# A linear-attention and mish feed-forward kernel: both feed-forward products by seven block products for eight, in two parts

## The chip, the cores and the metric

The kernel runs on one core of one Trainium2 chip. The time is the device time of one execution in microseconds (us); each kernel is run several times and the median stands. A profile of one execution goes with it. The engines are TensorE (PE, with its weight loads as PEld), VectorE (DVE), ScalarE (ACT), GpSimd (POOL) and SyncE (SP, which here issues all DMAs).

## What is computed

```python
kv = np.einsum('bhsd,bhse->bhde', k, v)                   # 8 batches, 8 heads, 576 rows, 64 wide
o = np.einsum('bhsd,bhde->bhse', q, kv)
o = o / np.sqrt(np.mean(o * o, axis=-1, keepdims=True) + 1e-06) * g_norm
x = o.transpose(0, 2, 1, 3).reshape(4608, 512)
h = x @ w_in                                              # 512 x 2048
sp = np.where(h > 20.0, h, np.log1p(np.exp(np.minimum(h, 20.0))))
out = (h * np.tanh(sp)) @ w_out                           # 2048 x 512
```

q, k, v and g_norm come as float32, w_in and w_out as float64. The output is float32.

## The kernel before

**Precision.** A float32 product runs as three float32r passes. Each operand is split into a high part (a rounded copy, made by ACT) and a low part (the rest, a subtraction on DVE); `split` at L84 does both. The passes are low by high, high by low and high by high, so every block of a product is three matmuls. The weights arrive as pairs of 32-bit words of a float64; `weight` (L92) makes a float32 of them with one ACT scaling and three DVE bit operations, and splits it. All of w_in and w_out, high and low, stays in SBUF.

**Tiles.** The 4608 tokens are 9 tiles of 512. For each tile and each of four head pairs, `unit_steps` (L191) loads q in strips of 32 by 32 (eight or sixteen DMAs for one or two batches in the tile), transposes it on DVE, multiplies it with the block-diagonal k^T v of the pair (L215 for the first two tiles, L218 to L220 with split operands for the rest), squares, sums over the head by a matmul with ones (L234, L236, L237), takes Ln and Exp for the inverse root (L242, L243) and scales (L246). k^T v of a batch is `kv_product` (L149), from two halves of four heads that `kv_load` (L122) brings.

**Feed-forward.** `hidden` (L255) makes one of 16 chunks of 128 hidden features for the 512 tokens: 12 matmuls, each with 128 x 128 weights standing and 512 tokens moving (L259 to L261). Mish has no instruction of its own here: `mish_a` and `mish_b` (L266 to L282) build it from Exp, a bounded minimum, Square, Ln, Exp and two multiplications, and split the outcome. `project_out` (L284) multiplies each chunk of 128 hidden features with w_out into four PSUM banks of 128 tokens by 512: 12 matmuls per chunk (L288 to L290), with the mish outputs standing and w_out moving. A tile is thus 384 matmuls of 512 columns, and the kernel 3456. After the 16th chunk the four banks are copied (L293) and stored (L294).

**Order.** The string `START` (L18) orders the first tile's x and the first weights. The main loop (L369) goes through 9 x 16 chunks; the second product runs two chunks behind the first. `attention_slots` (L337) puts the steps to the next tile's x between the chunks. In the first tile each chunk also loads and converts one piece of w_in, as far as any is left, and one of w_out (L376 to L380). Tile, the framework, takes this program with its dependencies and orders each engine's instructions by a simulated schedule, so an engine's queue may run ahead of the program's order. Buffers in SBUF and PSUM are rings of a given depth (`bufs`); an instruction that takes a buffer waits for the last reader of what was in it.

Of the kernel before, what the change touches and what calls it, by code (L numbers as in the profile page):

```python
# [12 lines left out]
LB = -18 * 0.6931471805599453     # log(4 2^-20)  # L13
# [4 lines left out]
START = (  # L18
    "w0 k0 q0 q1 m0 t1 w1 t0 q2 s1 s0 c0 c1 w2 k1 m1 "
    "n1 t2 w3 n0 c2 w4 q3 s2 n2 c3 t3 s3 c4 w5 c5 n3"  # L20
)
# [3 lines left out]
def linear_attention_rms_mish_ffn(  # L25
# [20 lines left out]
    w_in, w_out = w_in.bitcast(U32), w_out.bitcast(U32)   # words of float64, low first  # L46
    P = 128
    T = 512                      # tokens of one tile of the feed-forward part
    NT = NTOK // T
    NKC = DM // P                # contraction chunks of x w_in, = head pairs  # L50
    NFC = DF // P                # chunks of the hidden dimension
    NSUB = T // P
# [7 lines left out]
    stage = ctx.enter_context(tc.tile_pool(name="stage", bufs=2))  # L60
    wraw = ctx.enter_context(tc.tile_pool(name="wraw", bufs=3))
    wstage = ctx.enter_context(tc.tile_pool(name="wstage", bufs=2))
    kvp = ctx.enter_context(tc.tile_pool(name="kvp", bufs=1))
    att = ctx.enter_context(tc.tile_pool(name="att", bufs=1))
# [27 lines left out]
    def weight(src, hi, lo):  # L92
        w = wraw.tile([P, T, 2], U32, name="w64")
        nc.sync.dma_start(w.rearrange("p n t -> p (n t)"), src)

        low, high = w[:, :, 0], w[:, :, 1]
        x = wstage.tile([P, T], F32, name="w32")

        def scale():
# [336 lines left out]
```

## Time and profile before

| what | value |
|---|---|
| median of three runs | 923.93 us (923.43 to 924.76) |
| profiled execution's own time | 924.76 us |
| its span | 924.8 us |
| DMA | 55.31 MB, mean 60 GB/s |
| mean granted TensorE clock | 0.986 |

How to read it: busy times are those of one profiled execution. Matmuls are pipelined and their durations overlap, so the pace is the distance from one start to the next in the timeline. PEld is the loading of the standing operand and lies beside PE. Where a group's row ends in "idle before, releaser", the number is the time that the engine sat idle just ahead of such instructions and what ended it. The chain of waits follows the last instruction back to what released each step.

### The profile page before, as it was taken

The numbers are of one execution on the slowest core, as the hardware profiler recorded it, in microseconds if no ns is written. First come the engines' busy times: TensorE is split into PE (matmuls) and PEld (weight loads), VectorE is DVE, ScalarE is ACT, GpSimd is POOL, SyncE is SP. The second block draws the span as 40 slices with busy tenths as digits, with TensorE's granted clock in tenths as the row PEclk, the third lists the DMA queues.
The fourth block names the chain that finished last, engine by engine and source line by source line (L and its number), as shares of the span: only waits on it lengthen the run. The fifth ranks groups of instructions, "written<-read, shape, count | busy, mean of one in ns | idle before, by whom it ended". The sixth has DMA issues, their size and how long they took to land.

```text
span 924.8 us, 11829 instructions
## 1 busy us (share of the span) xinstructions
PE 896.3 (97%) x4348; PEld 717.2 (78%) x4348; DVE 539.0 (58%) x908; ACT 635.4 (69%) x1057; POOL 0.2 (0%) x4
## 2 busy tenths in 40 slices
PE   3789999999999999999999999999999999999997
PEld 1467778888888888888788878888888888888886
DVE  5889986565456544655466545554565456544443
ACT  3688877677667766776577666776676677766554
POOL 0000000000000000000000000000000000000000
PEclk9779999999999999999999999999999999999999
DMA  8964361200250005200430034002300030001001
GB/s 217 276 210 138 107 232 45 47 1 1 70 122 4 1 3 129 63 0 1 117 78 1 1 103 91 1 1 74 69 1 1 1 88 5 0 1 46 1 1 45
DMA packets 113434, 55.31 MB, mean 60 GB/s; under 512 B 88288, under 2 KB 104672, under 8 KB 113376
## 3 DMA queue, kind: packets, MB, share of 16 engines
q1 hardware_dynamic: 113376, 54.55, 21.4%
q8 instruction: 34, 0.56, 0.2%
q14 instruction: 24, 0.20, 0.1%
HBM read 45.09 MB, written 9.44 MB: 59 GB/s over the span
## 4 chain that ended last, share of the span: by engine, by line
PE 94%; DMA 3%; SPq 1%; DVE 1%; ACT 1%; issue 0%; ACTq 0%
PE psh L259 15%; PE acc L290 15%; PE acc L288 14%; PE acc L289 14%; PE psh L261 14%; PE psh L260 14%; PE psa L157 3%; DMA w<-in_moe_w_in_dram 2%; PE psa L220 1%; PE psa L219 1%; DMA vm<-in_v_dram 1%; PE psa L218 1%; SPq L185 1%; PE psa L237 1%; PE psa L236 1%; PE psa L215 1%
## 5 line engine op out<-in xcount | busy, mean ns | idle before, releaser
L259 PE MATMUL psh<-xh,wil 128*128 128x512 f32 x576 | 231.2, 402 | 2.2 <-ACT xh L85 2.2
L260 PE MATMUL psh<-xl,wih 128*128 128x512 f32 x576 | 228.2, 396 | 0.0
L261 PE MATMUL psh<-xh,wih 128*128 128x512 f32 x576 | 227.9, 396 | 0.0
L290 PE MATMUL acc<-woh,gh 128*128 128x512 f32 x576 | 227.6, 395 | 0.0
L289 PE MATMUL acc<-wol,gh 128*128 128x512 f32 x576 | 227.2, 394 | 0.0
L288 PE MATMUL acc<-woh,gl 128*128 128x512 f32 x576 | 223.4, 397 | 0.0
L86 DVE TENSOR_TENSOR gl<-n,gh 128x512 fp32r<-128x512 f32 x144 | 99.5, 691 | 84.7 <-ACT gh L85 81.5
L278 DVE TENSOR_TENSOR n<-u,n 128x512 f32<-128x512 f32 x144 | 99.3, 690 | 82.5 <-ACT n L274 82.3
L85 ACT CAST gh<-n 128x512 fp32r<-128x512 f32 x144 | 89.1, 618 | 82.2 <-DVE n L278 67.2
L272 DVE SCALAR_TENSOR_TENSOR u<-u,psh 128x512 f32<-128x512 f32 x144 | 98.8, 686 | 76.9 <-ACT n L271 76.8
L269 ACT ACTIVATE u<-psh 128x512 f32<-128x512 f32 x144 | 86.2, 598 | 78.6 <-PE psh L261 77.6
L259 PEld LDWEIGHTS psh<-xh,wil 128*128 128x128 f32 x576 | 108.9, 189 | 29.6 <-ACT xh L85 2.6
L260 PEld LDWEIGHTS psh<-xl,wih 128*128 128x128 f32 x576 | 109.1, 189 | 26.3 <-issue 0.9
L261 PEld LDWEIGHTS psh<-xh,wih 128*128 128x128 f32 x576 | 108.7, 189 | 25.8 <-issue 0.2
L289 PEld LDWEIGHTS acc<-wol,gh 128*128 128x128 f32 x576 | 108.5, 188 | 25.2 <-ACT u L269 0.4
L290 PEld LDWEIGHTS acc<-woh,gh 128*128 128x128 f32 x576 | 108.2, 188 | 25.4 <-issue 0.2
L288 PEld LDWEIGHTS acc<-woh,gl 128*128 128x128 f32 x576 | 108.2, 188 | 25.4 <-issue 0.4
L271 ACT ACTIVATE n<-u 128x512 f32<-128x512 f32 x144 | 90.8, 631 | 44.0 <-DVE u L270 42.9
L274 ACT ACTIVATE n<-n,lb 128x512 f32<-128x512 f32 x144 | 104.1, 723 | 3.6
L273 ACT ACTIVATE n<-n,tiny 128x512 f32<-128x512 f32 x144 | 104.1, 723 | 3.2
L270 DVE TENSOR_SCALAR u<-u 128x512 f32<-128x512 f32 x144 | 61.2, 425 | 68.9 <-ACT u L269 68.2
L86 DVE TENSOR_TENSOR fl<-fa,fh 128x512 fp32r<-128x512 f32 x56 | 38.6, 689 | 19.3 <-ACT fh L85 18.7
(61 smaller groups left out, 569.1 us busy)
## 6 DMA issues: line engine op xcount, KB each, us to landing
out_dram<-stg SPq DMA_DIRECT2D x36, 256.0 KB, 2.0
w<-in_moe_w_in_dram SPq DMA_DIRECT2D x16, 512.0 KB, 4.9
km<-in_k_dram SPq DMA_DIRECT2D x16, 512.0 KB, 4.0
vm<-in_v_dram SPq DMA_DIRECT2D x16, 512.0 KB, 5.4
w<-in_moe_w_out_dram SPq DMA_DIRECT2D x16, 512.0 KB, 3.9
stg<-in_q_dram SPq DMA_DIRECT2D x32, 64.0 KB, 2.4
stg<-in_q_dram SPq DMA_DIRECT2D x32, 56.0 KB, 2.0
stg<-in_q_dram SPq DMA_DIRECT2D x32, 48.0 KB, 1.9
```

The lines of the kernel that those rows point to most:

```text
L86: nc.vector.tensor_sub(lo, src, hi.bitcast(F32))
L259: nc.tensor.matmul(ps, wil[:, kc, f], xh[:, kc, :], start=(kc == 0), stop=False)
L260: nc.tensor.matmul(ps, wih[:, kc, f], xl[:, kc, :], start=False, stop=False)
L261: nc.tensor.matmul(ps, wih[:, kc, f], xh[:, kc, :], start=False, stop=(kc == NKC - 1))
L271: nc.scalar.activation(r, v, AF.Square, bias=1.0, scale=2.0)
L272: nc.vector.scalar_tensor_tensor(v, v, 0.5, ps, ALU.add, ALU.mult)
L273: nc.scalar.activation(r, r, AF.Ln, bias=tiny, scale=2.0 ** -20)
L274: nc.scalar.activation(r, r, AF.Exp, bias=lb, scale=-1.0)
L278: nc.vector.tensor_mul(r, v, r)
L288: nc.tensor.matmul(acc[t], gl[:, c], woh[:, fc, :], start=first, stop=False)
L289: nc.tensor.matmul(acc[t], gh[:, c], wol[:, fc, :], start=False, stop=False)
L290: nc.tensor.matmul(acc[t], gh[:, c], woh[:, fc, :], start=False, stop=last)
```

## The change

**The algorithm.** Both feed-forward products go by Strassen's way in Winograd's form. The two operands are cut in two by two blocks; four sums of blocks on each side give seven forms a side, and seven block products stand for eight. `PROD` names them: left form, right form, PSUM bank. The blocks accumulate partly in PSUM: a bank is copied aside by ACT while it holds one product (c1, c5, c2), the next product accumulates onto it, and DVE adds a copy to the finished bank.

**Part 1** runs over 9 tiles of 512 tokens, 4 groups a tile. A left form is 256 features by 256 tokens of x; a right form 256 features by 256 hidden ones of w_in. A block product is 12 matmuls of 256 columns, and 7 products make a group. x itself is now kept in float32, its sums are formed on DVE, and each form is split. The attention steps go by two head pairs at once (1024 elements an instruction) and k and v by two heads a load. Mish is one ACT instruction, `AF.Mish`; `in_turn` chains the Mish, Ln and Exp instructions in program order, with a table load ahead of each Ln. The mish outputs go to HBM (`gd`, 4608 x 2048 float32), two stores a group.

**The weights.** `weight_forms` makes seven split forms of a chunk. w_in is 8 chunks of 1024 elements a partition, kept in the eight buffers `wfp` of 14 KB a partition. w_out is 16 half chunks of 512, of which tiles 1 to 8 make two each; their forms are stored to HBM (`wod`, 14.7 MB).

**Part 2** begins when part 1's pools are closed. The eight buffers of w_in take w_out's forms. 18 groups of 256 tokens follow: one load of mish outputs (2.1 MB), four sums, seven forms, seven products of 24 matmuls of 256 columns each, and one store of 256 x 512 outputs. The forms are made three products ahead.

The core of the diff:

```diff
-    "w0 k0 q0 q1 m0 t1 w1 t0 q2 s1 s0 c0 c1 w2 k1 m1 "
-    "n1 t2 w3 n0 c2 w4 q3 s2 n2 c3 t3 s3 c4 w5 c5 n3"
+START = "k0 q0 k1 w0 m0 t0 q1 w1 s0 m1 t1 r0 s1 c0 r1 w2 a0 f0 f1 a1 f2 f3 f4 f5 c1 c2 w3"
+A11, S1, S2, S4, A12, S3, A22 = range(7)
+T1, T3, T2, T4, B11, B22, B21 = range(7)
+PROD = ((A11, B11, "a"), (S1, T1, "c"), (A22, T4, "p"), (S2, T2, "a"), (S4, B22, "c"), (A12, B21, "b"), (S3, T3, "a"))
...
+    wfp = ctx.enter_context(tc.tile_pool(name="wfp", bufs=NF2))
+    ps_m = ctx.enter_context(tc.tile_pool(name="ps_m", bufs=2, space=PSUM))
+    cp = ctx.enter_context(tc.tile_pool(name="cp", bufs=1))
+    ps_t = part1.enter_context(tc.tile_pool(name="ps_t", bufs=1, space=PSUM))
+    big = part1.enter_context(tc.tile_pool(name="big", bufs=3))
...
+    def mish(o, i):
+        in_turn(nc.scalar.activation(o, i, AF.Mish))
...
+        def join():
...
+            nc.vector.tensor_single_scalar(t, t, 3, ALU.logical_shift_left)
+            nc.vector.scalar_tensor_tensor(t, high, 0x80000000, t, ALU.bitwise_and, ALU.bitwise_or)
+            nc.vector.scalar_tensor_tensor(t, low, 29, t, ALU.logical_shift_right, ALU.bitwise_or)
+        def differences():
...
+            nc.vector.tensor_sub(d[:, 0:2], x[:, 1:3], x[:, 0:2])
+            nc.vector.tensor_sub(d[:, 2], x[:, 2], d[:, 0])
+            nc.vector.tensor_sub(d[:, 3], x[:, 3], d[:, 2])
...
+        def first():
+            parts(T1, T4 + 1, st["d"])
+        def rest():
+            parts(B11, B11 + 1, st["x"][:, 0:1])
+            parts(B22, B21 + 1, st["x"][:, 2:4])
...
+        def rstd():
+            r = st["r"] = att.tile([P, 2, T], F32, name="fa")
+            in_turn(nc.scalar.preload_act_table_set("natural_log_exp_and_others"))
+            in_turn(nc.scalar.activation(r, st["ss"], AF.Ln, bias=eps, scale=1.0 / D))
+            in_turn(nc.scalar.activation(r, r, AF.Exp, scale=-0.5))
...
+    def group(st, mm, copy_shape, put, prev):
...
+        def p0():
+            st["a"] = st["bank"]("a")
+            mm(st, st["a"], A11, B11, True)
+            st["c1"] = c_tile("c1")
+            nc.scalar.copy(st["c1"], st["a"])
+        def p1():
+            st["c"] = st["bank"]("bc")
+            mm(st, st["c"], S1, T1, True)
+            st["c5"] = c_tile("c5")
+            nc.scalar.copy(st["c5"], st["c"])
+        def p2():
+            if prev is not None:
+                mm(prev, prev["a"], A22, T4, False)
+                put(prev, "21", prev["a"])
+        def p3():
+            mm(st, st["a"], S2, T2, False)
+            st["c2"] = c_tile("c2")
+            nc.scalar.copy(st["c2"], st["a"])
+        def p4():
+            mm(st, st["c"], S4, B22, False)
+            put(st, "12", st["c"], st["c2"])
+        def p5():
+            st["b"] = st["bank"]("bc")
+            mm(st, st["b"], A12, B21, True)
+            put(st, "11", st["b"], st["c1"])
+        def p6():
+            mm(st, st["a"], S3, T3, False)
+            put(st, "22", st["a"], st["c5"])
...
+    def mm_in(st, bank, left, right, first):
+        xf = xs[st["i"]]["f"][left]
+        for jj in range(2):
+            w = wf[2 * st["n"] + jj]
+            for kc in range(2):
+                for s, (a, b) in enumerate(((1, 0), (0, 1), (0, 0))):
+                    nc.tensor.matmul(
+                        bank[:, jj], w[:, right, a, kc, :], xf[:, b, kc, :],
...
+    def put_in(st, block, bank, other=None):
...
+            st["u"] = big.tile([P, 4, T], F32, name="big")
...
+        if block == "21":
+            mish(left[:, :, TH:T], bank)
+            nc.sync.dma_start(gd[i][:, 2 * n:2 * n + 2, :], left)
+        elif block == "12":
+            nc.vector.tensor_add(right[:, :, 0:TH], bank, other)
+        elif block == "11":
+            nc.vector.tensor_add(left[:, :, 0:TH], bank, other)
+            mish(left[:, :, 0:TH], left[:, :, 0:TH])
+        else:
+            nc.vector.tensor_add(right[:, :, TH:T], bank, other)
+            mish(right, right)
+            nc.sync.dma_start(gd[i][:, NF2 + 2 * n:NF2 + 2 * n + 2, :], right)
...
+            for u, ns in enumerate(((3, 5, 6, 8, 9, 10), (10, 12, 13, 15, 16, 17))):
+                for s, n in enumerate(ns):
+                    slots[n].append(lambda u=u, s=s: units[u][s + 1]())
...
+    part1.close()
+    ps_u = ctx.enter_context(tc.tile_pool(name="ps_u", bufs=1, space=PSUM, reuse_waits="tile"))
+    gp = ctx.enter_context(tc.tile_pool(name="gp", bufs=2, reuse_waits="tile"))
+    sp = ctx.enter_context(tc.tile_pool(name="sp", bufs=1, reuse_waits="tile"))
+    fp = ctx.enter_context(tc.tile_pool(name="fp", bufs=5, reuse_waits="tile"))
+    op = ctx.enter_context(tc.tile_pool(name="op", bufs=2, reuse_waits="tile"))
+    wo = []
+    for c in range(NF2):
+        t = wfp.tile([P, 7, 2, G], F32R, name="wf")
+        nc.sync.dma_start(t.bitcast(F32), wod[c])
+        wo.append(t)
...
+    def mm_out(st, bank, left, right, first):
+        gf = st["f"][left]
+        for c in range(NF2):
+            for s, (a, b) in enumerate(((1, 0), (0, 1), (0, 0))):
+                nc.tensor.matmul(
+                    bank, gf[:, a, c, :], wo[c][:, right, b, :],
...
+    AHEAD = 3
```

More of the change, by code (lines that the diff above doesn't have):

```diff
@@ L48, in linear_attention_rms_mish_ffn @@
     T = 512
+    TH = T // 2
     NT = NTOK // T
@@ L51, in linear_attention_rms_mish_ffn @@
     NFC = DF // P
-    NSUB = T // P
+    NF2 = NFC // 2
+    NQ = NF2 // 2
+    G = 2 * P
+    NG = NTOK // G
     CM = 4
@@ L147, in kv_new, with kv_product @@
             kvl[b] = new(f"kvl{b % 2}", F32R) if first else kvl[b - 2]
-    def kv_product(b, half, km, kr, vm, vr):
-        ps = ps_a.tile([P, 2, D], F32, name="psa")
-        for i in range(2):
+    def kv_product(b, h0, nh, km, kr, vm, vr):
+        ps = ps_t.tile([P, nh // 2, D], F32, name="s2")
+        for i in range(nh // 2):
             for c in range(CM + 1):
@@ new lines, in put_out, with form_order @@
+    def put_out(st, block, bank, other=None):
+        if "o" not in st:
+            st["o"] = op.tile([P, 2, DM], F32, name="o")
+        o, s = st["o"], st["s"]
+        r, c = int(block[0]) - 1, int(block[1]) - 1
+        dst = o[:, r, c * G:(c + 1) * G]
+        if block == "21":
+            nc.scalar.copy(dst, bank)
+            nc.sync.dma_start(out[s * G:(s + 1) * G, :].rearrange("(h p) c -> p h c", p=P), o)
+        else:
+            nc.vector.tensor_add(dst, bank, other)
+    def form_order(s):
+        for g in range(s):
+            for left, _, bank in PROD:
+                if bank == "p":
+                    if g:
+                        yield g - 1, left
+                else:
+                    yield g, left
+        yield s - 1, A22
```

472 lines of the change are left out of this document (278 added, 194 removed).

## The prediction

> **What bounds the kernel now.** I read the page first: the engines' totals and the chain of waits.
>
> ```profile
> PE 896.3 (97%) x4348; PEld 717.2 (78%) x4348; DVE 539.0 (58%) x908; ACT 635.4 (69%) x1057; POOL 0.2 (0%) x4
> ...
> PE 94%; DMA 3%; SPq 1%; DVE 1%; ACT 1%; issue 0%; ACTq 0%
> ```
>
> The chain of waits that ended last is TensorE nearly from end to end, so shorter matmul work pays in full, as long as nothing else comes late in its place. Then the windows, cut where the first product of a tile starts. The columns are the stretch, its length, busy time and instruction count of PE, PEld, DVE, ACT and POOL, PE's granted clock, the DMA share and GB/s.
>
> ```profile
> 0.00:33.60 33.60, 15.59 (x94) 8.30 (x95) 19.84 (x40) 14.83 (x26) 0.20 (x4) 0.87 0.88 237
> 33.60:142.90 109.30, 103.75 (x537) 78.64 (x536) 101.77 (x188) 88.19 (x160) 0.00 (x0) 0.93 0.57 177
> 115.00:138.00 23.00, 23.00 (x143) 18.12 (x143) 20.63 (x41) 17.42 (x32) 0.00 (x0) 1.00 0.71 238
> 240.20:338.20 98.00, 98.00 (x498) 79.57 (x496) 53.45 (x88) 67.62 (x113) 0.00 (x0) 1.00 0.18 46
> 731.20:824.90 93.70, 93.70 (x405) 75.87 (x404) 52.47 (x84) 66.60 (x109) 0.00 (x0) 1.00 0.10 23
> ```
>
> A middle tile (fourth row) has PE busy all of its 98.0 us at full clock, ACT at 69%, DMA at 18%. The first tile (second row) is different: DVE is busy 101.77 of 109.3 us (93%) with weight conversion. So two stages have two limits, and I work out the new kernel by stages. Last I read the timeline of PE, where the distance of starts gives the pace; the durations overlap. At 512 columns:
>
> ```profile
> 400.94 0.39 PE L259 MATMUL psh<-xh,wil 128*128 128x512 f32 x1
> ...
> 403.72 0.39 PE L288 MATMUL acc<-woh,gl 128*128 128x512 f32 x1
> ```
>
> Twelve starts in 2.78 us: 0.2317 us each; 3456 of them are 801 us.
>
> **The products.** Seven for eight leaves 7/8 of the columns, but cut into matmuls of 256: a product is 12 matmuls in part 1 (36 groups of 7: 3024) and 24 in part 2 (18 groups of 7: 3024), 6048 in all. The trace shows 256 columns where the fifth tile's queries meet two batches' k^T v, half and half, each matmul with its own weight load:
>
> ```profile
> 366.84 0.28 PE L219 MATMUL psa<-fl,kvh 128*128 128x256 f32 x1
> 366.96 0.28 PE L220 MATMUL psa<-fh,kvh 128*128 128x256 f32 x1
> 367.08 0.28 PE L218 MATMUL psa<-fh,kvl 128*128 128x256 f32 x1
> 367.19 0.28 PE L219 MATMUL psa<-fl,kvh 128*128 128x256 f32 x1
> 367.31 0.28 PE L220 MATMUL psa<-fh,kvh 128*128 128x256 f32 x1
> 367.43 0.39 PE L260 MATMUL psh<-xl,wih 128*128 128x512 f32 x1
> ```
>
> Five starts in 0.59 us: 0.118 each. Would a long stream fall back to the pace of the weight loads? Shorter matmuls show what that pace is:
>
> ```profile
> 594.04 0.23 PE L218 MATMUL psa<-fh,kvl 128*128 128x128 f32 x1
> 594.10 0.28 PE L219 MATMUL psa<-fl,kvh 128*128 128x128 f32 x1
> 594.21 0.27 PE L220 MATMUL psa<-fh,kvh 128*128 128x128 f32 x1
> 594.32 0.44 PE L288 MATMUL acc<-woh,gl 128*128 128x512 f32 x1
> 594.61 0.39 PE L289 MATMUL acc<-wol,gh 128*128 128x512 f32 x1
> ```
>
> After one start at 0.06 the pace is 0.11, and the 512-column matmul behind them takes 0.29 where others take 0.23: loads that were fetched ahead are paid back. (0.06 + 0.11 + 0.11 + 0.06) / 3 is about 0.113 per load, so 256 columns, at 0.118, stand just above what the loads allow. I take 0.118 (bounds 0.113 and 0.120): 6048 x 0.118 = 714 us, 87 less than now, where a full eighth would be 100. A rule speaks against this: the Trainium skill, "TensorE: Matmul & The Clock Gate", section "The mechanism", says that weight loads overlap with running matmuls only when they use other row groups; all rows are used here. By it, with the page's 107 ns per load, the products alone would be an estimated 6048 x (0.107 + 0.107) = 1294 us and the whole 1451. The rows at 0.118 deny it.
>
> **Attention on PE** stays: 98.0 - 384 x 0.2317 = 9.0 us a tile, 93.7 - 89.0 = 4.7 where no k and v are left. Tiles 1 to 7 carry it: 6 x 9.0 + 4.7 = 58.7.
>
> **The first tile.** Before its first product two chunks of w_in must be seven forms, and by its end all eight. Prices, first from the groups by line, then two neighbours from the timeline:
>
> ```profile
> L205 DVE STREAM_TRANSPOSE fa<-stg 128x512 f32<-128x512 f32 x32 | 22.7, 708 | 7.9 <-DMA stg<-in_q_dram 7.6
> L246 DVE SCALAR_TENSOR_TENSOR fb<-psa,gcol,fb 128x512 f32<-128x512 f32 x32 | 23.9, 748 | 10.6 <-ACT fb L243 10.4
> L105 DVE SCALAR_TENSOR_TENSOR w<-w,w 128x512 uint32<-128x512 uint32 x32 | 21.9, 685 | 0.3
> L104 DVE TENSOR_SCALAR w<-w 128x512 uint32<-128x512 uint32 x32 | 13.5, 420 | 10.7 <-ACT w L100 10.3
> L86 DVE TENSOR_TENSOR wil<-w,wih 128x512 fp32r<-128x512 f32 x16 | 11.0, 688 | 0.9 <-ACT wih L85 0.7
> L166 DVE TENSOR_TENSOR kvl<-psa,kvh 64x128 fp32r<-64x128 f32 x28 | 8.0, 287 | 5.0 <-ACT kvh L165 4.7
> ```
>
> ```profile
> 121.57 0.69 DVE L86 TENSOR_TENSOR gl<-n,gh 128x512 fp32r<-128x512 f32 x1
> 122.17 0.68 DVE L86 TENSOR_TENSOR wil<-w,wih 128x512 fp32r<-128x512 f32 x1
> ```
>
> From 287 ns at 128 and 688 at 512 elements: 1.04 ns per element, so 0.42 us at 256 and 1.22 at 1024. A w_in chunk of 1024: shift 0.77, two joins 2.44, differences 0.69 + 2 x 0.42, low parts 1.22 + 0.42 + 0.69: 7.1, by eight 56.6. The first x (two transposes, two normalizations, four sums, seven low parts): 12.6; the second with its k^T v: 14.9; twelve additions out of PSUM: 8.3. Together 92.4 us. Packed instructions start 0.60 apart for 0.69 of duration: 80.4. At the 93% that DVE reached: 86.5. In the first 33.6 us it was idle for 13.8 (first window row). Tile 1 thus starts near 13.8 + 86.5 = 100; I take 102, for 142.9 now. Bounds: 82 (today's 33.6 plus a PE-bound tile of 48.6) and 114 (no packing). Converting w_out, which filled the first tile, moves to tiles 1 to 8 as two halves a tile, 4.2 us of DVE each: with 28.2 for additions, x and k^T v, 36.6 of 48.6 us. That is hidden as long as DVE has those 12 us to spare; its four loads and one store a half are counted in rival (4).
>
> **Part 1, tiles 1 to 8**: 8 x 336 x 0.118 = 317.2, plus 58.7. The old mish took four passes on ACT and three on DVE, all beside PE in a middle tile, so dropping them gains nothing by itself; it makes room for copies and additions. What could now be late is ACT:
>
> ```profile
> L269 ACT ACTIVATE u<-psh 128x512 f32<-128x512 f32 x144 | 86.2, 598 | 78.6 <-PE psh L261 77.6
> L85 ACT CAST fh<-fa 128x512 fp32r<-128x512 f32 x56 | 34.4, 615 | 18.5 <-DVE fa L205 14.3 <-PE psa L237 4.1
> L242 ACT ACTIVATE fb<-psa,eps 128x512 f32<-128x512 f32 x36 | 24.7, 686 | 1.1 <-PE psa L234 0.7 <-DVE xl L86 0.2
> L243 ACT ACTIVATE fb<-fb 128x512 f32<-128x512 f32 x36 | 22.7, 629 | 0.3
> L165 ACT CAST kvh<-psa 64x128 fp32r<-64x128 f32 x28 | 7.2, 257 | 7.1 <-DVE kvl L166 3.9 <-PE psa L157 3.0
> L72 ACT ACT_TABLE_LOAD x1 | 1.3, 1283 | 0.7 <-PEq L420 0.7
> ```
>
> 0.93 ns per element: 1024 take 1.07. The trace shows no Mish; the nearest rows are one pass of Exp from PSUM with no bias tile (598) and of Ln with one (686), and I take 598, as it has no bias tile either. Per tile: 12 copies 7.2; Mish 4 x 2.3; high parts 4.3; two units of Ln, Exp, square and two casts 10.8; k^T v 2.1; w_out 3.9: 37.5. Mish and Ln stand in different tables, so each of two units a tile switches there and back: 4 x 1.28 = 5.1. 42.6 of 48.6 us. A product accumulates onto a bank only after ACT copied what was in it, with two other products (2.8 us) to hide that. Queued behind a passage of load, Ln, Exp, load (1.28 + 1.16 + 1.10 + 1.28 = 4.8) a copy is up to 2.0 late, and the next product, with everything in PE's queue behind it, waits; 16 passages make 0 to 32 us. Below zero it can't go, since PE has no other slack in these tiles. I take 14, near the middle: copies need no table and may stand between the four.
>
> **Between the parts.** w_out's forms take over the memory of w_in's; the last two (3.7 MB) can start only when the last product of part 1 is done, and every product of part 2 needs all eight.
>
> ```profile
> out_dram<-stg SPq DMA_DIRECT2D x36, 256.0 KB, 2.0
> ```
>
> 238 GB/s at a share of 0.71 (window 115 to 138) is 335 at full: 11.0, plus 2.0 to land, plus 4 for a restart at a lower clock (0.93 in the first tile, where PE had idled): 17. The outputs of the first tile are long in HBM; their load and first form are hidden behind w_out's if they are issued by then. Bounds: 6, if the early chunks' matmuls run meanwhile and the rate is higher, and 50, if all 14.7 MB come late.
>
> **Part 2**: 3024 x 0.118 = 356.8. It is covered: per group of 19.8 us DVE has 11 x 1.22 + 3 x 0.42 = 14.7, ACT 7 x 1.07 + 4 x 0.38 = 9.0, DMA 2.1 MB, 6.3. **End**: last copy and store as now,
>
> ```profile
> 919.13 1.99 DMA out_dram<-stg
> ```
>
> with about 4.9 behind the last matmul. Sum: 102 + 317.2 + 58.7 + 14 + 17 + 356.8 + 4.9 = **870.6; I say 870**, against the profiled span of 924.8 (its own time 924.76; median 923.93, 0.1% less).
>
> **Rivals.** Two rows first: the duration of a weight load, and the issue of DMAs on SyncE.
>
> ```profile
> L218 PEld LDWEIGHTS psa<-fh,kvl 128*128 128x128 f32 x52 | 9.8, 188 | 1.3
> ```
>
> ```profile
> 364.32 4.48 SPq L185 DMA_DIRECT2D stg<-in_q_dram  x8
> 368.90 0.40 SPq L127 DMA_DIRECT2D km<-in_k_dram  x1
> 369.39 0.61 SPq L129 DMA_DIRECT2D kr<-in_k_dram  x1
> ```
>
> (1) Table passages hold PE: if ACT must also empty for as long as each load takes, a passage is 4.8 + 2.56 = 7.4, 4.6 late, 16 times: 73 instead of 14, 929: slower. It decides from a passage of 7.1 with no copy let between. For it speaks ACT at 88%. Against it: behind the one load of the trace no such time stands. The Trainium skill, "ScalarE: Activation LUTs", section "What ACT_TABLE_LOAD costs", puts a drain of 1380 ns beside the 1283; an estimate by it is 930; the 1283 agrees with the row, the drain no run here shows. (2) Weight loads set the pace after all: from 0.127 a matmul the gain is gone; at a load's duration in the row above the products take 6048 x 0.188 = 1137, and the whole about 1294. Five 256-column starts in a row speak against it, but a stream of thousands is not shown. The rule on row groups, above, has its small chance within this one's. (3) All w_out forms come late: 33 more, 903. (4) SyncE's queue: 66 transfers a tile (32 of q, 16 of k and v, 8 stores of mish outputs, 10 for w_out) at about 0.55 are 36 of 48.6 us. The 16 transfers of a q unit, twice the second row, hold back a store for 9 us; outputs, raw weights and forms share three buffers, so the next group's addition out of PSUM waits for one, and PE for its bank. 4 us a tile for 8 tiles: 902. For it: the queue works in order. Against: it runs ahead of need, as with k and v here, issued at 369 for the tile that starts at 338.2 + 98.0.
>
> **Chances.** Forecast 0.65 (850 to 890), (1) 0.07, (2) 0.02, (3) 0.12, (4) 0.14. Within 0.2%, about what a measurement of this kernel tells from no change, 0.01, taken from (1); slower 0.08; faster 0.91. The range takes in (3) and (4) with some more stalls, and below the forecast the low ends of stalls (0 for 14) and of the boundary (6 for 17): 845 to 912; beyond it are (1), (2) and mixtures, under 2 in 10.
>
> **What would show it.** 3024 matmuls of 256 columns on each of the two lines, starting 0.118 apart; first tile with DVE over 90% and tile 1 near 102; PE busy through tiles 1 to 7 with waits on ACT's copies of some 2 us a tile; one PE gap of 13 to 17 us near 495, released by w_out's forms; part 2 without gaps, 357 long. A pace of 0.125 or more, or part 1 ending past 530, would prove it wrong.

## The result and the profile after

The changed kernel takes 986.52 us (median of four runs, 985.29 to 987.35), the kernel before 924.35 beside it (923.43 to 925.07): a ratio of 1.0666, 95% interval 1.065 to 1.0681. It is slower by 62 us where 54 us faster was forecast. The profiled span is 985.5 us. First the totals of the engines, the granted clock in forty slices and the chain of waits, from the page:

```profile
PE 854.9 (87%) x6940; PEld 820.8 (83%) x6940; DVE 593.6 (60%) x805; ACT 508.2 (52%) x758; POOL 0.2 (0%) x4
...
PEclk9699989998998979989799975999999999999999
...
PE 63%; DMA 11%; SPq 9%; ACT 8%; issue 5%; DVE 3%; ACTq 0%; DVEq 0%
```

TensorE's busy time is 41 us less than before (854.9 for 896.3), so the products did get cheaper. But the chain is TensorE for 63% only, for 94% before; DMA, SyncE's queue and ScalarE have come in, and the clock falls in many slices. The windows, cut at the stages of the prediction's sum (columns as there; a tile is counted as 336 matmuls of the first feed-forward product), say where:

```profile
0.00:34.90 34.90, 18.91 (x96) 8.73 (x97) 11.95 (x20) 10.32 (x14) 0.20 (x4) 0.88 0.87 209
34.90:138.10 103.20, 72.59 (x538) 61.93 (x537) 78.95 (x120) 63.07 (x103) 0.00 (x0) 0.84 0.55 152
138.10:585.20 447.10, 397.50 (x3286) 384.92 (x3284) 246.04 (x414) 282.64 (x442) 0.00 (x0) 0.94 0.60 186
357.40:367.60 10.20, 5.60 (x26) 5.60 (x27) 9.65 (x17) 10.17 (x17) 0.00 (x0) 0.50 0.62 222
547.00:603.00 56.00, 30.46 (x221) 29.76 (x219) 9.80 (x18) 12.61 (x21) 0.00 (x0) 0.79 1.00 376
585.20:615.40 30.20, 0.42 (x3) 0.15 (x2) 2.48 (x3) 2.69 (x3) 0.00 (x0) 0.56 0.99 342
615.40:981.10 365.70, 365.18 (x3024) 364.98 (x3024) 254.14 (x250) 149.08 (x195) 0.00 (x0) 0.99 0.36 118
```

| term | forecast | measured | difference |
|---|---|---|---|
| tile 1 starts (rows 1 and 2) | 102 | 138.1 | +36.1 |
| tiles 1 to 8 (row 3) | 317.2 + 58.7 + 14 = 389.9 | 447.1 | +57.2 |
| gap between the parts (row 6) | 17 | 30.2 | +13.2 |
| part 2 (row 7) | 356.8 | 365.7 | +8.9 |
| end | 4.9 | 4.4 | -0.5 |

The differences add up to 114.9, which is 985.5 - 870.6. In part 2 TensorE is busy for all but half a microsecond, at 365.7 / 3024 = 0.121 a matmul. Tiles 1 to 8 are another thing: TensorE is idle for 447.1 - 397.5 = 49.6 us. And in those stages the granted clock is 0.50 for 57.2 us in eight stretches, of which the fourth row is one: right around a stop the same matmuls take twice as long (24 starts from 362.00 in 5.5 us, 0.23 each). TensorE is busy in 37.6 of those 57.2 us, so half of that, 18.8, is lost. What is left, 397.5 - 18.8 = 378.7 us, is the work at full clock; 2688 x 0.120 + 58.7 = 381.3 was to be expected at the pace measured.

The stops have one place, the start of each of tiles 3 to 7 (3.1 + 3.2, 5.5, 7.3, 6.6 and 7.1 us from one start to the next in the timeline of PE), with shorter ones at the start of tile 8 (2.6) and in it (4.2 and 4.5). The waits of the whole execution (total, times, longest) and the chain that ends the stop at 355 to 362 us (start, length):

```profile
DVE wx L135 <- ACT wx L130: 40.2, 15, 5.7
...
PE a L405 <- ACT big L107: 32.7, 11, 7.1
```

```profile
354.01 0.44 SPq L125
354.45 0.04 issue
354.49 2.38 DMA big<-in_moe_w_out_dram
...
356.97 0.66 ACT wx L130
357.63 0.95 ACT fa L317
358.58 0.02 issue
358.60 1.28 ACT L107
359.88 0.01 issue
359.89 2.07 ACT big L107 x3
...
362.00 4.21 PE a L405 x18
```

TensorE waits for Mish, since the next product goes into a PSUM bank that Mish (L107) still has to read. Mish waits in ScalarE's queue behind the scaling of a raw w_out half (L130), which waits for its transfer, then behind the Exp of the root (L317) and the load of Mish's table. So two chains meet in one queue: w_out's data, and the root with its tables. No engine is short of time here (ScalarE is busy for 63% of row 3); what stands ahead in its queue makes the stop.

### The profile page after: what moved, and what is told of

Same layout as the page of the kernel before. It is cut to its first block, busy times and chain, and to the rows that moved or that the text cites. A ratio compares the mean times of both kernels' runs of the same rounds, so it can differ in the third digit from the quotient of the medians.

```text
span 985.5 us, 17006 instructions
## 1 busy us (share of the span) xinstructions
PE 854.9 (87%) x6940; PEld 820.8 (83%) x6940; DVE 593.6 (60%) x805; ACT 508.2 (52%) x758; POOL 0.2 (0%) x4
## 3 DMA queue, kind: packets, MB, share of 16 engines
q1 hardware_dynamic: 204896, 159.42, 52.3%
## 4 chain that ended last, share of the span: by engine, by line
PE 63%; DMA 11%; SPq 9%; ACT 8%; issue 5%; DVE 3%; ACTq 0%; DVEq 0%
PE a L591 21%; PE bc L591 16%; PE a L405 13%; PE bc L405 9%; SPq L262 5%; DMA gd<-big 4%; ACT big L107 3%; DMA vm<-in_v_dram 2%; ACT L107 2%; DMA big<-in_moe_w_out_dram 2%; PE s L230 2%; SPq L125 2%; DMA wod<-big 2%; SPq L195 1%; ACT fa L317 1%
## 5 line engine op out<-in xcount | busy, mean ns | idle before, releaser
L405 PE MATMUL a<-xf,wf 128*128 128x256 f32 x1728 | 252.0, 298 | 45.3 <-ACT big L107 32.7
L405 PEld LDWEIGHTS a<-xf,wf 128*128 128x128 f32 x1728 | 234.4, 205 | 52.7 <-ACT big L107 34.7
L591 PE MATMUL a<-wf,gf 128*128 128x256 f32 x1728 | 215.8, 285 | 30.3 <-issue 29.8
L591 PEld LDWEIGHTS a<-wf,gf 128*128 128x128 f32 x1728 | 212.2, 194 | 30.8 <-issue 30.0
L405 PE MATMUL bc<-xf,wf 128*128 128x256 f32 x1296 | 183.2, 291 | 9.9 <-DVE big L420 5.2
L405 PEld LDWEIGHTS bc<-xf,wf 128*128 128x128 f32 x1296 | 171.0, 199 | 14.1 <-DVE big L420 7.1
L591 PE MATMUL bc<-wf,gf 128*128 128x256 f32 x1296 | 161.4, 283 | 0.0
L591 PEld LDWEIGHTS bc<-wf,gf 128*128 128x128 f32 x1296 | 158.1, 192 | 0.0
L111 DVE TENSOR_TENSOR gf<-g,gf 128x1024 fp32r<-128x1024 f32 x72 | 87.8, 1221 | 46.0 <-ACT gf L110 46.0
L110 ACT CAST gf<-g 128x1024 fp32r<-128x1024 f32 x72 | 75.6, 1050 | 54.1 <-PE bc L591 27.4
L110 ACT CAST gf<-s 128x1024 fp32r<-128x1024 f32 x54 | 56.6, 1048 | 66.0 <-PE a L591 31.2
L111 DVE TENSOR_TENSOR gf<-s,gf 128x1024 fp32r<-128x1024 f32 x54 | 66.1, 1223 | 27.3 <-ACT gf L110 27.3
L107 ACT ACTIVATE big<-big 128x512 f32<-128x512 f32 x72 | 58.3, 839 | 21.2 <-DVE big L422 10.9
L420 DVE TENSOR_TENSOR big<-bc,c 128x512 f32<-128x512 f32 x36 | 24.8, 689 | 49.4 <-PE bc L405 29.6
L111 DVE TENSOR_TENSOR fl<-fa,fh 128x1024 fp32r<-128x1024 f32 x28 | 34.2, 1222 | 31.1 <-ACT fh L110 30.7
L382 ACT COPY c<-a 128x512 f32<-128x512 f32 (+1 forms) x54 | 27.8, 515 | 34.1 <-PE a L591 28.1
L577 DVE TENSOR_TENSOR s<-g 128x1024 f32<-128x1024 f32 x18 | 22.0, 1223 | 36.3 <-DMA g<-gd 36.2
L135 DVE TENSOR_SCALAR wx<-wx 128x512 uint32<-128x512 uint32 (+1 forms) x24 | 12.3, 512 | 40.2 <-ACT wx L130 40.2
L239 DVE TENSOR_TENSOR kvl<-s,kvh 64x64 fp32r<-64x64 f32 x56 | 12.4, 221 | 38.4 <-ACT kvh L238 37.2
L130 ACT ACTIVATE wx<-big 128x512 f32<-128x512 f32 (+1 forms) x24 | 19.9, 829 | 29.6 <-DMA big<-in_moe_w_out_dram 29.6
## 6 DMA issues: line engine op xcount, KB each, us to landing
wf<-wod SPq DMA_DIRECT2D x8, 1792.0 KB, 12.8
```

The costliest lines, as they stand in the source:

```text
L107: in_turn(nc.scalar.activation(o, i, AF.Mish))
L110: nc.scalar.copy(hi, src)
L111: nc.vector.tensor_sub(lo, src, hi.bitcast(F32))
L130: nc.scalar.mul(st["x"], st["w"][:, :, 1].bitcast(F32), 2.0 ** -112)
L382: nc.scalar.copy(st["c2"], st["a"])
L405: nc.tensor.matmul(bank[:, jj], w[:, right, a, kc, :], xf[:, b, kc, :], start=first and jj == kc == s == 0, stop=(kc == 1 and s == 2), ski ...
```

## The experiments

Each kernel was timed by one execution, and the kernel before took 924.4 to 927.3 us beside them, so differences of some 3 us say little. Each edit also lets the framework order the queues anew. The columns, all from the profile: the chip's span, where tile 1 starts, how long tiles 1 to 8 take, TensorE's idle time in them, what halved clock costs in them (half of the time that TensorE is busy at 0.50), and the gap between the parts.

| kernel | span | tile 1 | tiles 1-8 | idle | clock | gap |
|---|---|---|---|---|---|---|
| changed | 985.5 | 138.1 | 447.1 | 49.6 | 18.8 | 30.2 |
| e1 w on GpSimd's queue | 980.4 | 139.9 | 441.3 | 43.1 | 18.6 | 28.6 |
| e2 own raw buffer | 980.7 | 136.8 | 444.3 | 50.5 | 13.9 | 30.1 |
| e3 q on GpSimd's queue | 1012.0 | 159.6 | 452.5 | 56.6 | 16.6 | 29.2 |
| e4 pools of part 2 moved | 984.0 | 137.0 | 446.2 | 51.9 | 15.2 | 23.5 |
| e5 no root, no order | 955.2 | 132.0 | 423.7 | 34.6 | 8.7 | 29.6 |
| e6 no table switch | 959.3 | 133.5 | 424.6 | 34.1 | 12.8 | 31.2 |
| e7 root later | 978.2 | 132.7 | 445.2 | 49.2 | 14.4 | 30.5 |
| e8 no joins | 976.8 | 115.8 | 461.1 | 56.5 | 19.3 | 30.2 |
| e9 w_out in tile 1 alone | 959.7 | 139.1 | 417.6 | 26.9 | 12.3 | 32.9 |
| e10 that, and no root | 930.0 | 132.9 | 392.9 | 10.0 | 1.7 | 34.6 |
| e11 four moves, all computed | 973.2 | 138.3 | 432.6 | 39.3 | 12.9 | 18.6 |
| e12 early data, no root | 943.1 | 137.6 | 401.3 | 18.4 | 3.0 | 34.1 |
| e13 q in long pieces | 978.5 | 134.2 | 443.9 | 49.0 | 16.0 | 30.7 |
| e14 half the forms | 968.1 | 136.4 | 446.0 | 51.2 | 15.7 | 15.1 |
| e15 that, pools moved | 975.2 | 138.0 | 448.4 | 52.3 | 17.4 | 11.2 |
| e16 four terms | 902.7 | 107.3 | 404.5 | 13.7 | 5.2 | 13.5 |
| e17 q in few issues | 971.0 | 127.5 | 443.0 | 47.5 | 16.3 | 30.5 |
| e18 five terms | 881.2 | 107.0 | 386.5 | 5.0 | 0.0 | 17.0 |

**First theories: a queue, a buffer, the rate (e1 to e4).**

```diff
 e1 -nc.sync.dma_start(t[:, i]..., src)          +nc.gpsimd.dma_start(t[:, i]..., src)
 e2 +wrp = tc.tile_pool(name="wrp", bufs=1)      raw halves of w_out from wrp, not from big
 e3 -nc.sync.dma_start(t[32 * i:...], q[...])    +nc.gpsimd.dma_start(...)
 e4 -gp, sp, fp, op(bufs=2)                      +sp, op(bufs=3), gp, fp
```

> Loads of w_in and w_out are issued by GpSimd instead of SyncE; nothing else is changed. Theory queue (the stop of 5.5 to 7.3 us at the start of every tile comes of w_out's loads standing behind q's transfers in SyncE's queue, and the first tile's 103 us of w_in's loads standing there too): stops under 2 us at the starts of tiles 3 and 4, first tile 85 to 95 us long, the half clock gone from most of part 1, total 920 to 950. Rival ring (the loads wait for one of three shared buffers): the stops stay at 5 us or more, total 970 to 990. Rival tables (table loads and the Ln and Exp between them hold the copies): stops stay, total 980 to 990.

> The raw w_out halves get a buffer of their own, so that their loads no longer wait for one of the three buffers they share with mish outputs and forms. Queue: stops stay in the tiles whose chain shows q's transfers (starts of tiles 3, 4), total 965 to 985. Ring: the waits of w_out's loads on stores of forms (13.6 us) and of outputs (5.7 us) go and all stops fall under 2 us, total 930 to 950. Tables: 980 to 990.

> q's loads (32 a tile) are issued by GpSimd instead of SyncE. Queue: the same as with the weights moved, or better, since k, v and stores are relieved too: total 915 to 945, first tile 80 to 95 us. Ring: 965 to 985, the stops whose chain shows only a store's landing (starts of tiles 2 and 5) stay. Tables: 980 to 990.

> Only the order of part 2's pools is changed, so that the buffers of loaded mish outputs lie on memory that is free before part 1 ends, not on the buffers of its last stores. Theory landing (the gap of 30.2 us is w_out's last forms, then the last store landing behind them, then the load of outputs): the gap falls to 12 to 17 us, total 968 to 974. Rival rate (the gap is the time that all the bytes take whatever their order): gap 25 to 30, total 981 to 986.

e1, e2 and e4 give 5.1 us or less, and e3 loses 26.5. With the raw weights off SyncE's queue the stops at the tiles' starts shrink to 3.5 to 4.5 us but stay: their chain is then the root's alone. A buffer of its own for the raw halves leaves them at 4 to 6, some of them in two pieces. So rival (4) of the prediction, SyncE's queue and the three shared buffers, is not the cause as long as only one of the two is mended; what both are worth together, without the root, is seen at e12. q on GpSimd's queue makes things worse: the first product starts at 66.7 us for 34.9. e4 shortens the gap by 6.7 us and gives it back as a stall in the first group (29.56 us for 22.33); what it says of the cause is taken up at e15.

**The root's chain (e5 to e7).**

```diff
 e5 -preload; in_turn(Ln); in_turn(Exp)   +activation(r, ss, Square); activation(r, r, Square)
 e6 -preload; in_turn(Ln); in_turn(Exp)   +in_turn(Mish); in_turn(Mish)
 e7 -(10, 12, 13, 15, 16, 17)             +(10, 12, 13, 15, 19, 20); x_sums at 20, 21 for 18, 19
```

> Ln and Exp of the inverse root become two Square passes of the same shape, with no table load and not in the chain that orders Mish behind them (the root is thus not formed). Theory order (every tile's stop comes of the Mish instructions that stand in ACT's order behind the next x's Ln and Exp, which wait for their sums): no stop over 2 us at the starts of tiles 3 to 7, half clock after the first tile under 15 us, those tiles 49 to 53 us, total 930 to 950. Rival loads (the two table loads a unit take ACT's time): the same here. Rival late data (w_out's raw loads and k, v come late to ACT's queue, whatever stands behind): stops of 3 us or more stay, total 965 to 985.

> Ln and Exp become two Mish passes of the same shape, so no table is switched, but they stay in the chain that orders all Mish after them (the root is not formed). Theory order: the stops stay, shorter by one load of 1.3 us, about 2 to 6 us; half clock stays 35 us or more; total 965 to 980. Rival loads: the stops go as without the chain, total 930 to 950. Rival late data: as without the chain, 965 to 985.

> The inverse root and normalization of the second unit stand three products later in the program (19 and 20 for 16 and 17), the two pairs of sums of x two later; all is computed. Theory order: fewer Mish instructions stand behind a Ln that waits, stops fall by 2 us or more, total 955 to 975. Rival loads: 980 to 990. Rival late data: 975 to 990.

Idle and clock together are 68.4 us in the changed kernel, 43.3 in e5, 46.9 in e6. e6 keeps two passes in the same chain ahead of the Mishes and drops the switch of tables, and brings 21.5 of e5's 25.1. So most of the gain comes with dropping the loads. How it comes is not shown: only one load, 1.28 us, stands in the chain of the stop above, and e6's queue is also ordered otherwise (w_out's L130 runs at 341.43, ahead of both passes; in the changed kernel it stands between Ln and Exp). Neither theory's time is met by e6 (961.09; the order wanted 965 or more, the loads 930 to 950), and stops of 2.7 to 5.8 us stay at the tiles' starts, as the theory of the order had it. Stops stay in e5 too (956.94, between its two cases), and their chain there is w_out's data:

```profile
276.54 7.05 DMA wod<-big
...
284.95 3.12 DMA big<-in_moe_w_out_dram
...
288.17 0.66 ACT wx L130
288.83 0.47 ACT c L365
289.30 0.96 ACT big L107
```

A raw half may be loaded only when the store of an older half has left the shared buffer; ScalarE holds L130 at the head of its queue meanwhile, and Mish behind it. e7 moves the root and leaves that chain: stops of 4.1 to 6.5 us stay, and its 980.04 is what its two rivals wanted (980 to 990 and 975 to 990).

**Both chains (e9 to e12).**

```diff
 e9  -if outs:                  +if i == 1:       (and wod[0] is read for each of wod[c])
 e10 e9 and e5
 e11 e1, e2, e4 and e7
 e12 e1, e2 and e5
```

> Only tile 1 converts blocks of w_out here; later tiles convert none, and part 2 reads the first block's forms for all four groups (so the sums that w_out enters are not computed). The chain of the root (squares, sums, Ln, Exp, table load, the Mishes behind them) is as in the changed kernel. Theory of two chains: the stops at the tiles' starts stay at about 3.6 us, as in the run with w_out's loads on GpSimd's queue, each with 3.4 to 6.8 us of halved clock behind it; tiles 1 to 8 take 425 to 440 us for 447, the whole 960 to 975. Rival, the data of w_out alone makes the stops: none over 2 us, tiles 1 to 8 390 to 405, the whole 925 to 945.

> The run before this one, and the root replaced by two passes of Square that stand in no order with the Mishes and load no table (the root is not formed). Both chains are gone. Theory of two chains: no stop over 2 us at a tile's start, no halved clock between the first tile's end and 540 us, TensorE's idle time in tiles 1 to 8 down from 49.6 to 10 to 20 us, tiles 1 to 8 385 to 400 us for 447 (the prediction's term was 390), the whole 920 to 940. Rival, the engines' own pace behind TensorE: idle time of 30 us or more stays in small pieces, tiles of 52 to 56 us, tiles 1 to 8 415 or more, the whole over 950.

> All of the computation: raw weights issued by GpSimd, a buffer of their own for w_out's raw halves, unit 1's root three slots later, part 2's pools laid out so that its first loads of g wait for no Mish output. Theory of two chains: with the data early and the root later the stops shrink to 2 us or less and the halved clock to under 25 us; tiles 1 to 8 405 to 420 us for 447, the whole 940 to 960; the boundary stays at about 30 us in all, its loads being bound by the rate. Rival, the root's place does not matter and the chain of its sums stays: stops of 3.6 us and 45 us of halved clock as with GpSimd's queue alone, the whole 975 to 985.

> w_out is converted in every tile, its raw halves in a buffer of their own and issued by GpSimd; the root is replaced by two passes of Square outside the order of the Mishes (the root is not formed). Theory of two chains: the data come early and no root stands before the Mishes, so the stops go as in the run with neither chain: none over 2 us before 540 us, tiles 1 to 8 390 to 405 us, the whole 925 to 945. Rival, early issue does not make the data early (the transfers share the rate with q, k, v and the Mish outputs): stops of 3 to 6 us stay at w_out's scale, as in the run without the root alone, tiles 1 to 8 415 to 424, the whole 950 to 957.

In e9 the stops at the starts of tiles 3 to 7 are 3.5 to 4.5 us, by the root's chain. This is the one that ends at 350 us:

```profile
344.37 1.13 ACT fa L316
...
346.59 1.28 ACT L107
347.88 0.01 issue
347.89 2.07 ACT big L107 x3
349.96 0.04 issue
350.00 1.01 PE a L405 x3
```

e9's tiles were better than expected (417.6 for 425 to 440), perhaps because w_out's conversion takes ScalarE's and VectorE's time as well; that was not tried apart. With both chains gone, in e10, tiles 1 to 8 take 392.9 us, one stop of 2.9 us is left, and the clock stays up:

```profile
132.90:525.80 392.90, 382.85 (x3285) 370.27 (x3284) 193.88 (x288) 225.79 (x356) 0.00 (x0) 1.00 0.50 156
```

The rival, the engines' pace, wanted 415 or more. Idle and clock fall by 25.1 (e5), by 29.2 (e9) and by 56.7 (e10): the two chains add. e12 converts every half of w_out, with the data early, and comes to 401.3 and 943.1. That is 8.4 us more in tiles 1 to 8 than e10 without the conversion, and two stops, of 2.8 and 4.6 us, stay where none over 2 was expected. Beside e5, which also has no root, early data bring 21.9 us of idle and clock (21.4 for 43.3), where the queue alone had brought 6.7 (e1) and the buffer alone 4.0 (e2) with the root in place. Whether it takes both for the data to come early, or the root's chain covered a part, was not tried apart. e11 has all of the computation and falls short of what was expected: 432.6, since the root's chain (sums, Ln, Exp, table, Mish) is still there three slots later, with stops of about 3 us and one of 5.5; one of 8.7 us comes in tile 8, where VectorE waits for a store of Mish outputs that takes long to land. Its gap of 18.6 is followed by two stalls of 5.2 and 5.7 us. At 975.04 it is the best version found that computes everything, and it doesn't reach the kernel before.

**The first tile (e3 above, e8, e13, e17).**

```diff
 e8  +if m == 1: around the two joins, so that w_in's are left out
 e13 q[b, h, s0 + (i % 2) * n // 2 : ..., :] in place of 32-wide columns: same issues, long pieces
 e17 two issues a stretch of rows (64 partitions, two heads) for eight
```

> Two of the bit operations on each of w_in's eight chunks (2.4 us of DVE each) are left out, so w_in's forms are not those of w_in. Theory DVE (the first tile is paced by DVE's conversion of w_in, 91 us of work until tile 1 starts): tile 1 starts at 115 to 123 instead of 138. Rival issue (the first tile is paced by SyncE's issue of q, k, v and w_in): tile 1 starts at 132 to 138.

> The same bytes of q in the same number of issues on SyncE's queue, but taken as contiguous stretches of rows (256 to 2048 bytes a piece, for 128): the values land in another order, so the output is that of a shuffled q. Theory, q's small pieces make VectorE's waits in tile 0 and crowd the other loads: the first product at 28 to 31 us for 34.9, tile 1 starts at 120 to 130 for 138.1, idle VectorE in that stretch down by 8 us or more, the whole 955 to 975. Rival, what costs is the issue of many transfers one after the other and the work on VectorE: tile 1 starts at 134 to 139, the whole 978 to 987.

> q comes in a quarter of the issues (2 for each stretch of rows and unit, for 8), each a contiguous stretch of rows with 64 partitions and two heads, so q is shuffled; bytes as before. Theory, the 0.47 us that SyncE takes for each of q's issues, 8 to 16 in a row, hold tile 0 (4.4 us ahead of the transfer at 38.7, and two runs of 14 and 15 us with the other loads later): the first product at 26 to 31 us for 34.9, tile 1 starts at 118 to 129 for 138.1, and the whole is 955 to 972, the tiles' stops a little shorter. Rival, VectorE's own chain holds tile 0 and the queue only shares the blame: tile 1 starts at 132 to 138, the whole 976 to 987.

```profile
31.10:115.80 84.70, 64.64 (x466) 54.89 (x467) 61.45 (x102) 60.51 (x96) 0.00 (x0) 0.90 0.60 161
```

```profile
33.80:127.50 93.70, 71.92 (x536) 61.75 (x537) 79.20 (x122) 61.49 (x102) 0.00 (x0) 0.87 0.53 163
```

The first row is e8, the second e17. Without the joins VectorE's busy time up to tile 1 falls by 21.2 us (from 90.90 to 69.75) and tile 1 starts 22.3 earlier, with the idle time unchanged (46.0 for 47.2): VectorE's work is on the path about one for one. But tiles 1 to 8 are 14.0 longer, and 8.7 us are left at the end. e13 shows that q's 128-byte pieces are not what holds the tile: 134.2, as the rival said. The number of issues has a part in it: with a quarter of them (and longer pieces as well) tile 1 starts at 127.5, 10.6 earlier, and VectorE's idle time falls from 47.2 to 36.3 us. The first product came at 33.8, though, for an expected 26 to 31, and the whole, 972.77, just misses its range. The chain of the changed kernel shows the issues from inside: nine issues in a row, a transfer, VectorE's transpose, and soon the next run.

```profile
34.26 0.42 SPq L262
...
38.16 0.48 SPq L262
38.68 2.00 DMA qs<-in_q_dram
40.76 0.05 DVEq L276
40.86 0.17 DVE fh L276
...
45.69 5.14 DMA qs<-in_q_dram
```

**The boundary (e4 above, e14, e15).** Part 2's eight buffers are allocated as four, each standing for two blocks; e15 is that with e4's pools.

```diff
-for c in range(NF2): ... wo.append(t)      +for c in range(NF2 // 2): ... wo += [t, t]
```

> Part 2 loads four of the eight buffers of w_out forms and uses each for two blocks of the sum: 7.3 MB at the boundary for 14.7 (half of w_out's forms are left out). Theory, the boundary is bound by the rate at which the forms come: the last Mish output lands in 3 to 5 us after its issue for 12 to 15, the gap between the products of the two parts falls from 30.2 to 10 to 18 us, the stops in tile 8 (4.2 and 4.5 us) to 2 or less; the whole 960 to 972. Rival, the chain of buffers (last store, then g into the place of the buffer that it reads, then the sums): the gap stays at 27 to 31 us, the whole 980 to 986.

> The run before this one, and part 2's pools laid out so that g's first buffers do not lie on the Mish outputs' (half of w_out's forms are left out). With the rate out of the way the chain of buffers is what is left: if both set the gap, it falls to 3 to 8 us here, the first group takes 21 to 23 us, and the whole is 950 to 962. Rival, the last store and g's load do not matter once the rate is free: gap and first group as in the run before, within 3 us.

```profile
582.40:597.50 15.10, 0.40 (x2) 0.12 (x2) 2.44 (x3) 2.69 (x3) 0.00 (x0) 0.61 0.85 287
```

Half of the bytes bring half of the gap: 15.1 us (e14's window above) for 30.2, and the last two Mish outputs land in 3.3 and 2.6 us. In the changed kernel the forms' loads begin near 547 us and DMA is full until 603 (fifth row of the windows after: 56.0 us at 376 GB/s are 21 MB, of which the forms are 14.7). The timeline at the end of it shows what that does to the first load of Mish outputs, which goes into the place of the last buffer and so has to wait for that buffer's store:

```profile
590.84 0.40 SPq L418 DMA_DIRECT2D gd<-big  x1
593.97 0.32 SPq L556 DMA_DIRECT2D wf<-wod  x1
602.57 4.45 SPq L567 DMA_DIRECT2D g<-gd  x2
612.92 1.04 ACT L110 CAST gf<-g 128x1024 fp32r<-128x1024 f32 x1 [26.68 <-DMA g<-gd]
```

One part of what was expected of e14 missed: the stops in tile 8 stay (4.2 and 4.9 us). e15 missed too, and its chain shows why, and why e4 had proved less than it seemed to: the pools were moved so that the sums now lie on the Mish outputs' buffer. The wait had moved, and was not gone:

```profile
589.32 13.09 DMA gd<-big
...
602.53 1.24 DVE s L577
```

So the rate is shown for half of the gap. For the other 15 us e14's timeline has the chain of buffers: the last store, issued at 583.46, lands at 586.1, the Mish outputs are loaded into its place, and only then come the sums.

```profile
586.21 2.82 SPq L567 DMA_DIRECT2D g<-gd  x2
595.06 1.23 DVE L577 TENSOR_TENSOR s<-g 128x1024 f32<-128x1024 f32 x1 [15.24 <-DMA g<-gd]
```

How much of it a layout free of this chain would save was not tried.

**All terms (e16, e18).** Both take out the joins, w_out after tile 1, the root and half of the forms; e16 has e4's pools, e18 the changed kernel's pools and q in few issues.

> All four terms that the prediction missed are taken out together: w_in's joins (two of three passes), w_out's conversion in all tiles but the first, the root with its tables (two passes of Square in its place), half of the forms' loads and the overlaid pools. If the terms add up: tile 1 starts at 108 to 118 us, tiles 1 to 8 take 388 to 398, the gap 3 to 8, part 2 365 to 367, the whole 872 to 895. If they hide one another (what is taken away at one place is waited for at the next, as with the joins alone, where 16 of 22 us were lost again by tile 3): over 905.

> As the run with the four terms, but with part 2's pools where the changed kernel has them, and q in a quarter of the issues (left out or altered: two of three join passes, w_out's conversion after tile 1, the root, half of the forms, q's order). The run with four terms gave 902.7 on the chip's clock, with 13.5 us of gap and 8.9 of stall in the first group. If q's issues are a term of tile 0 of their own: first product 24 to 28 us, tile 1 starts at 94 to 102, tiles 1 to 8 388 to 400, gap and first stall 15 to 19 us, the whole 875 to 890, which is the prediction's 870.6 within the pace of part 2. If they hide behind the rest: tile 1 starts at 104 to 108, the whole 893 to 902.

e16 ended at 902.7, between its two cases, with the pools' stall among it. e18, by stages:

```profile
0.00:107.00 107.00, 82.70 (x608) 65.41 (x609) 69.85 (x121) 66.30 (x110) 0.20 (x4) 0.90 0.70 203
107.00:493.50 386.50, 381.48 (x3310) 369.97 (x3308) 195.76 (x291) 228.68 (x361) 0.00 (x0) 1.00 0.48 161
493.50:510.50 17.00, 0.30 (x4) 0.09 (x2) 2.45 (x3) 2.69 (x3) 0.00 (x0) 0.57 0.79 268
510.50:876.60 366.10, 365.58 (x3023) 365.38 (x3024) 254.66 (x250) 149.21 (x195) 0.00 (x0) 0.99 0.36 120
```

Tiles 1 to 8 take 386.5 for the 389.9 of the prediction (5.0 us of it idle, where 14 were taken, and a pace 0.002 slower), and there is no halved clock in them. The gap is 17.0 for 17, but that is chance: half of all the forms come here, and not the last two alone. Tile 1 starts at 107.0, no earlier than in e16 (107.3), so beside the other changes q's issues bring nothing to that start, as the rival had it; VectorE is idle there for 37.2 us though 21 us of its work are gone. But tiles 1 to 8 are 18.0 us shorter than in e16, where only q's issues differ up to the boundary: what they didn't bring at one place they brought at the next, and the whole is within the 875 to 890 of the first case.

## Why the prediction was wrong, step by step

- **Products and pace: right.** 3024 matmuls on each line, 0.120 to 0.121 a start; 0.118 was taken, 0.120 was the bound given. At 0.120 that is 6.0 of the 8.9 us of part 2, whose first group takes 2.2 more than the others, and 2688 x 0.002 = 5.4 in tiles 1 to 8. Weight loads don't set another pace (rival 2).
- **"The first tile ... tile 1 thus starts near 100; I take 102": failed**, by 36.1 us, and outside its own bounds (82 to 114). The 92.4 us of VectorE's work before packing look right beside the 90.9 that were busy (11.95 + 78.95), but partly by luck: the durations of its 140 instructions up to tile 1 add up to 97 us, and their overlap takes 6 off. "Packed instructions start 0.60 apart" took 12 off, to 80.4. Work missed and overlap that didn't come are 10.5 us together. And the idle time was taken from a kernel that had other work to fill its waits: 13.8 ahead of the first product and 6.1 more at 93% make 19.9, measured are 22.95 + 24.25 = 47.2. e17 takes 10.9 of these 27.3 us off with fewer issues of q on SyncE. The other 16 are open; the profile puts further waits of VectorE there on a load of w_in (10.3 us) and on ScalarE's copies of w_in's forms (6.8 us). Together 10.5 + 27.3 = 37.8, from the 100.3 worked out (102 taken) to 138.1.
- **"Queued behind a passage ... 16 passages make 0 to 32 us. I take 14": failed**, by 35.6 us of idle time and 18.8 of clock. The passage was priced right, in kind and in its parts (Ln 1.11 and Exp 1.06 for 1.16 and 1.10, the load 1.28). Three things were missed. It was priced for a copy that happens to be queued behind a passage, where Mish itself stands behind it by the order that the kernel writes, and TensorE behind Mish. w_out's raw halves were counted as ScalarE's and VectorE's work ("hidden as long as DVE has those 12 us to spare"), not as a wait for a transfer at the head of ScalarE's queue (e9: 29.2 us, with the conversion's work). And a stop was priced at its own length.
- **Rival (4)**, at 32 us, had the late transfers by SyncE's queue and the shared buffers, and so one of the two chains. It let them hold VectorE's additions out of PSUM; in the chain of the stop they hold ScalarE's scaling of w_out (L130), and Mish behind it. With both mended and no root it is worth 21.9 us (e12 beside e5).
- **Rival (1)** came near in size by chance (73 us; 68.4 of idle and clock measured), for the mechanism is another: no drain beside the table load is there. In the chain of the stop Exp ends at 358.58, the load runs from 358.60 to 359.88 and Mish begins at 359.89. The Trainium skill, "ScalarE: Activation LUTs", section "What ACT_TABLE_LOAD costs", has a drain of 1380 ns beside its 1283; the 1283 agrees with the rows, the drain these rows don't show. The prediction's estimate of 930 by it should be 933 by its own terms: 4.8 + 2.76 - 2.8 = 4.8 us a passage, 16 times, in place of 14. The rows of the loads and of Mish from PSUM:

```profile
L315 ACT ACT_TABLE_LOAD x18 | 23.1, 1283 | 1.0 <-PEq L675 0.7
L107 ACT ACT_TABLE_LOAD x17 | 21.8, 1283 | 4.5 <-DVE big L422 4.3
L107 ACT ACTIVATE big<-a 128x512 f32<-128x512 f32 x36 | 21.2, 588 | 16.3 <-PE a L405 16.2
```

- **Mish by one pass: right**, 588 ns from PSUM for the 598 taken.
- **"Between the parts ... 17": failed** by 13.2, inside its bounds (6 to 50). It counted the last 3.7 MB only and took the earlier forms as there. All 14.7 MB come within the last 38 us of part 1 and the gap, beside the Mish outputs, at a full DMA; with half the bytes the gap is 15.1 (e14), and 17.0 in e18. Rival (3) had this cause, and priced it at 33 more.
- **Part 2 without gaps, and the end: right.**
- **The proof of error was named**: part 1 past 530 us. It ended at 585.

The terms themselves were sound where nothing waits. The forecast failed in what lies between engines, and all three misses have the same sign.

## What to carry to other kernels

Price an in-order queue by what stands at its head: a small pass that waits for a transfer, or a table load, costs everything behind it, even on an engine that is half idle. When the bounding engine gets faster, its stops cost more than their length where the clock falls behind them (18.8 us beside 49.6 here), so a forecast needs the number of stops and not only their sum. A share of busy time read from one kernel can't be carried to another with other work in that stage.

## What the runs showed of the hardware

- **The halved clock.** Around each stop at the starts of tiles 3 to 8 of the changed kernel the granted clock is 0.50 for 3.4, 6.8 or 10.2 us, beginning 2.4 to 4 us after the stop began. A stop of 2.6 us (at 527.4) brought 3.4 us of it, one of 7.3 us (at 354.7) 10.2; in e5 one of 2.9 us (at 229.7) brought none. The kernel before ran at 1.00 in its middle tiles. The Trainium skill, "TensorE: Matmul & The Clock Gate", section "HAM oscillation — how this bites in real kernels", warns of idle gaps over some 3.4 us; the halving and the multiples of 3.4 agree, but shorter stops were enough here, though not always.
- **Many small issues on SyncE cost time.** Each of q's issues takes 0.42 to 0.48 us of SyncE's queue. The same bytes in longer pieces, in as many issues, moved the start of tile 1 by 3.9 us; a quarter of the issues moved it by 10.6, but by nothing where VectorE had 21 us less to do (e18 beside e16).
- **A full DMA holds stores back.** With the forms' loads in the queues (from 548 us) a Mish output of 512 KB took 10 to 16 us to land, where the median was 2.9 in the first tile.
